# A two-stage FFT feeding a SoLU layer on one core: another order for the opening (x between the halves of w_in, Q in long rows, r by one-column products)

## The chip, the cores and the metric

The kernel runs on one core of one Trainium2 chip. The metric is the device time of one execution in microseconds (us), lower is better; the median of three runs is taken. One further execution was recorded by the profiler, and all views below come from it.

## What is computed

`x` is 8 x 3136 x 256 (float32). The first stage takes the real part of its two-dimensional FFT over the last two axes; the second treats the 25088 rows of the result as tokens of a SoLU layer:

```python
X = np.fft.fft(np.fft.fft(x, axis=1), axis=2).real      # 8 x 3136 x 256, then 25088 x 256
h = X @ w_in                                            # w_in 256 x 1024
e = np.exp(h - h.max(-1, keepdims=True))
solu = h * e / e.sum(-1, keepdims=True)
ln = (solu - mean(solu)) / sqrt(var(solu) + 1e-6) * g_ln
out = ln @ w_out                                        # w_out 1024 x 256
```

`w_in` and `w_out` arrive as float64. [...]each weight is loaded as two 32-bit words and put together on the core: the exponent is taken from the high word and clamped, the significand is formed from both words, and the two are multiplied into a float32.

## The kernel before, in words

**Tiling.** The sequence of 3136 = 49 x 64 is transformed in two steps. The batch of 8 is worked on as 4 pairs. For a pair, `load` (L108 on) brings in x in 8 chunks, c = 0 to 7: the rows `xa` by a direct load issued from SyncE (SP), L117, and the mirrored rows `xb` by an indirect load (gather) issued from GpSimd (POOL), L119. Each of the two is 98 partitions x 4 KB, 392 KB. VectorE (DVE) adds the mirror (`add_mirror`, L134 and L136) and folds the features (`fold`, L141, L142, L154) into `y`. TensorE (PE) multiplies `y` by the table `F` (`transform1`, L208), ScalarE (ACT) copies the result to `z` (L211), and SP stores it to a DRAM scratch `zd` (`keep`, L216), from where it is loaded again with the partitions in another order as `g` (`turn`, L224).

A **unit** is one of 100 sets of 128 or 256 tokens: one value of k1 (25 of them) in one of 4 pairs. For each unit `transform2` (L236) makes `q` (ACT copies it, L242), and `up` (L264) multiplies `q` by the combined weight `Wi` = Q w_in, where Q is the feature-FFT table. One feature column needs a rank-one term: `even` (L270) adds `w_mid` times a per-token scalar `r` to the product. `r` is one row of `q` laid over the 128 partitions; `spread` (L247) does that by a DMA that SP issues. Then follow, all on 128 x 1024 tiles: `join` (L278, DVE, twice: tokens k and mirrored k), `expo` (L286, ACT), `product` (L293, DVE), `square` (L300, ACT), a transposition, and the product with `w_out` (`down`, L468, or from unit 5 on a product of seven block products, L401).

**The weights.** Before the first unit can run, `w_in` must have been converted and multiplied by Q: `Wi` and `w_mid` come from `product_in(h)`, h = 0, 1, 2 (L601: four 128 x 512 matrix products each, two halves of the columns times two chunks of the depth). `w_in` is loaded and converted in four pieces of 128 x 512 (`piece_in` L504; `exponent_in` L507 and, on ACT, `confine` L529 to L531; `narrow_in` L507, L543, L546, L551). `w_out` is loaded in two halves (`load_out`, L613) and converted in four pieces (`exponent_out`, `narrow_out`, the same lines), with `g_ln` multiplied in at L551. `centre` (L631 to L633) then takes the mean out of `Wo`, and `weight_sums` (L377) makes the sums for the seven-product form.

**What sets the order.** The whole is in a manual schedule: each engine executes its instructions in the order in which the program text issues them. The opening is written out by hand (L672 to L758): idx and identity; piece 0 of w_in, then pieces and x chunks in turn, `F` after piece 1; Q and g_ln after x chunk 3 (g_ln as 128 x 8 single elements, Q as 2 x 257 elements for each partition); then for each chunk c the conversion of a piece (c = 0, 1, 2), the fold, the load of chunk c + 6, and the transform; `product_in(0)` after chunk 3; w_out, `load_table(0)` and `mid` in chunk 3's turn. Chunks 6 and 7 go to the two buffers that chunks 0 and 1 used, so their gathers wait for those folds. After the last chunk come the loads of `g`, the rest of the weights, units 0 to 3 (which use plain transposition on PE, `whole = 4`), and unit 4 as the first of the block-transposed form. From unit 6 on the loop repeats in a fixed pattern.

A compiled DMA signals its end on one of eight semaphores that SP uses in turn: in the compiled order of the SP queue each DMA waits for the one eight places before it.

Of the kernel before, what the change touches and what calls it, by code (L numbers as in the profile page):

```python
# [17 lines left out]
P = 128  # L18
# [10 lines left out]
KG = 5  # L29
# [6 lines left out]
def kernel(  # L36
# [139 lines left out]
    def transform1(pr, s):  # L176

        c, l = divmod(2 * s, CH)  # L180
        if s == 0:
            pr.zd = dram.tile([ZR, NH, D], FP32, tag="zd", name="zd")
        if l == 0:

            if pr.p or c < 2:
                pr.z = zpool.tile([ZR, CH, D], FP32, tag="z", name="z")
            elif c < 4:
                if c == 2:
                    pr.z_u = fpool.tile([P, 2, FF], FP32, tag="u", name="z_u", bufs=1)
                pr.z = pr.z_u[0:ZR, c - 2].rearrange("p (l d) -> p l d", l=CH)  # L190
            elif c < 6:
                pr.z = Ws.rearrange("p (h w) c k -> h p (w c k)", h=2)[c - 4, 0:ZR].rearrange("p (l d) -> p l d", l=CH)
            elif c == 6:
                pr.z = S_tiles[1][0:ZR, 0:2].rearrange("p a c k -> p (a c k)").rearrange("p (l d) -> p l d", l=CH)
            else:
                pr.z = gpool.tile([P, KG, D], FP32, tag="g", name="z_g")[0:ZR, 0:CH, :]
            pr.zs[c] = pr.z
        y = pr.y[c]
        ps = result(0 if pr.p else s).rearrange("p (l d) -> p l d", l=2)
        if s == NH // 2 - 1:  # L200
            parts = [(ps[0:ZR, 0], y[:, l], 0), (ps[0:ZR, 1], pr.y0[:, 0], 1), (ps[0:ZR, 1], y[:, l + 1], 2)]
        else:
            parts = [(ps[0:ZR], y[:, l : l + 2], 0)]
        pr.done.append(s)
        first = True
        for o, i, t in parts:
            for h, cs in enumerate((EVEN, ODD)):
                nc.tensor.matmul(o[..., cs], F[:, 2 * t + h, :], i[..., cs], start=first, stop=True,  # L208
                                 skip_group_check=True)
                first = False  # L210
        nc.scalar.copy(pr.z[:, l : l + 2, :], ps[0:ZR])  # L211
        if l == CH - 2:
            keep(pr, c, slice(0, ZR if pr.p else 4 * KG))
# [29 lines left out]

    def spread(t):

        t.r = small.tile([P, 1], FP32, tag="r", name="r")
        nc.sync.dma_start(out=t.r, in_=t.q[0:1, P : 2 * P])  # L247

    class Unit:


        def __init__(self, p, k1):
            self.p, self.k1 = p, k1
            self.signs = (0, 1) if k1 else (0,)
            self.h, self.u, self.ot = [None] * 2, [None] * 2, [None] * 2

    def up(t, c):
# [259 lines left out]
    def confine(unit, here=False):  # L519
# [11 lines left out]
        nc.scalar.activation(out=unit, in_=u, func=ACT.Identity, bias=limits[:, 2:3], scale=-(2.0 ** 23))  # L531

    def narrow(w, raw, outs, unit):

        if w.dtype == FP32:
            for o, scale in outs:
                nc.vector.tensor_scalar(out=o, in0=o, scalar1=scale, scalar2=2.0 ** 20, op0=ALU.mult, op1=ALU.mult)
            return
        lo, hi = raw[:, 0 : 2 * NW : 2], raw[:, 1 : 2 * NW : 2]

        bits(mantissa, hi, 0xFFFFF, ALU.bitwise_and, 0x100000, ALU.bitwise_or)
        m = lo.bitcast(FP32)
        nc.vector.scalar_tensor_tensor(out=m, in0=lo.bitcast(U32), scalar=2.0 ** -32, in1=mantissa, op0=ALU.mult,  # L543
                                       op1=ALU.add)

# [8 lines left out]
    class Weights:  # L554


        def load_in(self):
            raw = fpool.tile([P, 2, FF, 2], FP32, tag="v", name="raw_in", bufs=2)
            raw = raw.rearrange("p a f b -> p (a f b)").bitcast(I32)
            self.w_in = [fpool.tile([P, FF], FP32, tag="h", name="w_in", bufs=2) for _ in range(KD)]  # L560
            self.pieces, self.units = [], []
            for c in range(KD):
                for j in range(0, FF, NW):
                    i = 2 * (c * FF + j)
# [4 lines left out]

        def exponent_in(self, i):  # L570
            w, raw, o, c, j, n = self.pieces[i]
            self.units.append(exponent(w, raw))
            confine(self.units[-1])

# [4 lines left out]
        def load_tables(self):  # L579
            self.Q = fpool.tile([P, KD, D + 1], FP32, tag="ev", name="Q", bufs=1)  # L580
            nc.sync.dma_start(out=self.Q, in_=q_tab.rearrange("(c p) d -> p c d", p=P))
            nc.sync.dma_start(out=g_ln, in_=moe_g_ln.rearrange("(c p) -> p c", p=P))

# [5 lines left out]
        def mid(self):  # L589

            self.m = w_mid[:, 0 : KD * P].rearrange("p (c k) -> p c k", c=KD)
            for c in range(KD):
                nc.scalar.mul(out=self.m[:, c, :], in_=ones, mul=self.Q[:, c, D:])

        def product_in(self, h):
            ps = ps_h.tile([P, FF], FP32, tag=f"h{h % 2}", name="wps")
            for half in range(2):
                fs = slice(half * HW, (half + 1) * HW)
                for c in range(KD):
                    lhsT = self.m[:, c, :] if h == KD else self.Q[:, c, h * P : (h + 1) * P]  # L600
                    nc.tensor.matmul(ps[:, fs], lhsT, self.w_in[c][:, fs], start=(c == 0), stop=(c == KD - 1))  # L601
            nc.scalar.copy(w_mid if h == KD else Wi[:, h, :], ps)

# [12 lines left out]
        def scale_out(self):  # L616
            nc.scalar.mul(out=g_ln, in_=g_ln, mul=2.0 ** -20)

        def exponent_out(self, i):
            self.units.append(exponent(moe_w_out, self.raw[:, 2 * i * NW : 2 * (i + 1) * NW]))  # L620

        def narrow_out(self, i):
# [48 lines left out]
    with tc.manual_schedule():  # L671
# [6 lines left out]
        for c in range(2, 6, 2):  # L678
            room = fpool.tile([P, 2, KF, 4, 64], FP32, tag="uT", name="room", bufs=2)
            room = room[0:PR].rearrange("p w c i m -> p (w c i m)").rearrange("p (a n) -> p a n", a=4)  # L680
            rooms[c], rooms[c + 1] = [room[:, i] for i in (0, 1)], [room[:, i] for i in (2, 3)]
        weights.load_in()
        for c in range(4):
            weights.piece_in(c)
            if c:
                load(first, c - 1, rooms.get(c - 1))
            if c == 1:
                nc.sync.dma_start(out=F, in_=f_tab)
        load(first, 3, rooms[3])
        weights.load_tables()  # L690
        for c in range(4, 6):
            load(first, c, rooms[c])
        nc.vector.memset(ones, 1.0)
# [4 lines left out]
        for t in T:  # L698
            nc.vector.memset(t, 0.0)
        weights.exponent_in(0)  # L700
        weights.exponent_in(1)
        for c in range(NC):

            if c == 0:
                weights.narrow_in(0)
                weights.narrow_in(1)
            elif c < 3:
                weights.narrow_in(c + 1)
            if c < 2:
                weights.exponent_in(c + 2)  # L710
            add_mirror(first, c, nc.vector)
            fold(first, c)
            if c == NC - 1:
                for i in range(3):
                    weights.exponent_out(i)
            if c + 6 < NC:
                load(first, c + 6)
            if c == 3:
                weights.place_out()
                for i in range(2):  # L720
                    weights.load_out(i)
                weights.load_table(0)
                weights.mid()
                weights.scale_out()
            for s in range(CH // 2):
                transform1(first, c * CH // 2 + s)
            if c == 3:
                weights.product_in(0)

        turn(first, 0, nc.sync, 0, 2)  # L730
        turn(first, 0, nc.gpsimd, 2, KG)

        confine(weights.units[0], True)
        for i in range(1, 3):
            confine(weights.units[i])
        weights.product_in(1)
        weights.narrow_out(0)
        weights.exponent_out(3)
        weights.product_in(2)
        for i in range(1, 3):  # L740
            weights.narrow_out(i)

        units = [Unit(p, k1) for p in range(NP) for k1 in range(NK)]
        for t in units[:2]:
            take2(t, transform2(pairs[0], t.k1))
            spread(t)
        confine(weights.units[-1])
        for c in (2, 3, 0, 1, 4, 5, 6, 7):
            keep(first, c, slice(4 * KG, ZR))
        weights.load_table(1)  # L750
        lag = 5
        whole = 4

        def second_transform(i):
            if i < len(units):
                t = units[i]
                take2(t, transform2(pairs[t.p], t.k1))
                spread(t)  # L758

# [6 lines left out]
        def begin(i):  # L766

            cur = units[i]
            enter(i)
            even(cur, up(cur, 0))  # L770
            cur.odd = up(cur, 1)
# [7 lines left out]
        batches = []  # L779
        begin(0)  # L780
        for i in range(whole + 1):
# [14 lines left out]
            if i == 0:  # L796

                weights.narrow_out(3)
            for s in cur.signs:
# [112 lines left out]
def _tables(B, S, D):  # L912
# [13 lines left out]
    for t, (u, v) in enumerate(tabs):  # L926
# [18 lines left out]
    rows = np.arange(B)[:, None, None] * S + (N1 - np.arange(1, NK)) + N1 * np.arange(N2)[::-1, None]  # L945
    mirror[:, B // 2 * NC :] = rows.reshape(B // 2, P, NK - 1).transpose(1, 0, 2).reshape(P, -1)
    return {
        "f_tab": f.reshape(PR, 6, ZR).astype(np.float32),
# [37 lines left out]
```

## Time and profile before

| what | us |
|---|---|
| median of three runs (lowest, highest) | 1158.69 (1158.67, 1158.85) |
| profiled execution: own time | 1157.6 |
| profiled execution: span of the core | 1155.8 |
| outside the span in that execution | 1.8 |
| PE busy in the span | 1109.1 (96%) |
| DVE busy | 1013.8 (88%) |
| POOL busy | 848.0 (73%) |
| ACT busy | 758.3 (66%) |
| x of the first pair folded (start of L507 behind the last L154) | 46.68 |
| first `even` (L270), of unit 0 | 59.62 |
| `even` of unit 2 | 77.95 |
| first of the PE instructions that then follow each other to the end | 113.84 |

How to read it: busy times are sums over the whole span, so they say little of the first 114 us, where this change lies. Times of single events are counted from the start of the span. "Chain of work that ended last" is a path that the profile follows back from the last instruction, at each step to what released it. A DMA queue named q1 is the one that SP issues to, q0 the one that POOL issues to; both run on the same 16 DMA engines.

### The profile page before, as it was taken

How to read it: one execution, taken by the hardware profiler on the slowest of the kernel's cores; microseconds unless marked ns; L12 is line 12 of the kernel's file. 1: busy time of each engine (PE TensorE's matmuls, PEld its weight loads, DVE VectorE, ACT ScalarE, POOL GpSimd, SP SyncE). 2: the span in 40 equal slices, each digit the busy share in tenths (PEclk: the TensorE clock that was granted, in tenths of full speed). 3: DMA queues.
4: the chain of work that ended last, by engine and by line, in shares of the span. 5: the costliest groups of instructions: out<-in, count | busy, mean ns of one | idle time of the engine just before them, and what ended most of it. 6: DMA issues, size and time to landing. Idle time of an engine off the chain costs nothing.

```text
span 1155.8 us, 21664 instructions
## 1 busy us (share of the span) xinstructions
PE 1109.1 (96%) x7026; PEld 888.2 (77%) x7026; DVE 1013.8 (88%) x1440; ACT 758.3 (66%) x1725; POOL 848.0 (73%) x742
## 2 busy tenths in 40 slices
PE   2888999999999999999999999999999999999998
PEld 1555787888887778878887778878778788888887
DVE  7879988888999998888899998888898999898883
ACT  4567667666665766666666766666666676676661
POOL 3035888865898988866689888877499596777764
PEclk9999999999999999999999999999999999999999
DMA  9771798766998779866969697876697675865664
GB/s 238 204 192 39 168 191 195 184 145 145 160 187 160 180 177 184 198 138 143 164 139 204 150 189 171 203 175 141 149 159 146 137 163 122 150 144 111 139 135 111
DMA packets 458479, 185.75 MB, mean 161 GB/s; under 512 B 425750, under 2 KB 440350, under 8 KB 458368
## 3 DMA queue, kind: packets, MB, share of 16 engines
q1 hardware_dynamic: 444608, 146.22, 61.2%
q0 software_dynamic: 13760, 38.16, 12.4%
q8 instruction: 57, 0.93, 0.3%
q14 instruction: 54, 0.44, 0.1%
HBM read 44.78 MB, written 38.80 MB: 72 GB/s over the span
## 4 chain that ended last, share of the span: by engine, by line
PE 81%; DMA 5%; SPq 4%; DVE 4%; issue 2%; POOL 2%; ACT 1%; POOLq 0%; DVEq 0%; ACTq 0%
PE ps_m L401 48%; PE ps_h L264 25%; PE ps_m L208 4%; PE ps_m L236 3%; SPq L365 3%; DMA room<-in_x_dram 2%; DMA uT<-v 1%; DVE h L278 1%; POOL S L394 1%; DMA r<-q 1%; DVE u L293 1%; DMA F<-in_f_tab_dram 1%; SPq L216 1%; PE ps_m L468 1%; PE wps L601 1%
## 5 line engine op out<-in xcount | busy, mean ns | idle before, releaser
L264 PE MATMUL ps_h<-Wi,q 128*128 128x512 f32 x800 | 362.0, 594 | 7.9 <-DVE nmax L278 4.8
L394 POOL TENSOR_TENSOR S<-uT 128x512 f32<-128x512 f32 x186 | 251.1, 1350 | 104.6 <-DMA out_dram<-ot 40.9
L300 ACT ACTIVATE h<-u,usum 128x1024 f32<-128x1024 f32 x196 | 225.2, 1149 | 139.9 <-DVE u L293 139.9
L401 PE MATMUL ps_m<-Ws,S 128*128 128x128 f32 x2304 | 298.7, 276 | 4.3 <-issue 3.0
L401 PEld LDWEIGHTS ps_m<-Ws,S 128*128 128x128 f32 x2304 | 280.8, 192 | 8.8 <-issue 3.3
L264 PEld LDWEIGHTS ps_h<-Wi,q 128*128 128x128 f32 x800 | 144.0, 190 | 155.3 <-issue 139.9
L293 DVE SCALAR_TENSOR_TENSOR u<-h,u 128x1024 f32<-128x1024 f32 x196 | 259.4, 1359 | 0.8 <-ACT u L286 0.7
L286 ACT ACTIVATE u<-h,nmax 128x1024 f32<-128x1024 f32 x196 | 223.6, 1143 | 15.8 <-DVE nmax L278 11.8
L336 DVE STREAM_TRANSPOSE v<-u 128x2048 f32<-128x2048 f32 x93 | 215.5, 2317 | 3.2
L401 PE MATMUL ps_m<-Wo,uT 128*128 128x128 f32 x1536 | 213.1, 282 | 0.0
L401 PEld LDWEIGHTS ps_m<-Wo,uT 128*128 128x128 f32 x1536 | 197.3, 197 | 0.9 <-issue 0.9
L394 POOL TENSOR_TENSOR S<-uT,S 128x512 f32<-128x512 f32 x93 | 133.1, 1431 | 7.3
L278 DVE CUSTOM_DVE_ANT_0 h<-ev,ps_h 128x1024 f32<-128x1024 f32 x100 | 122.1, 1221 | 17.3 <-DVE ev L270 7.9
L479 POOL DMA_INDIRECT out_dram<-ot,idx x96 | 111.2, 1158 | 33.5 <-issue 16.6
L394 POOL TENSOR_TENSOR S<-S,uT 128x512 f32<-128x512 f32 x93 | 126.6, 1362 | 7.3
L278 DVE CUSTOM_DVE_ANT_0 h<-h,ps_h 128x1024 f32<-128x1024 f32 x96 | 117.3, 1221 | 14.2 <-ACT ot L444 0.5
L270 DVE SCALAR_TENSOR_TENSOR ev<-w_mid,r,ps_h 128x1024 f32<-128x1024 f32 x100 | 124.0, 1240 | 4.2 <-DMA r<-q 2.3
L401 PE MATMUL ps_m<-Ws,uT 128*128 128x128 f32 x768 | 106.2, 281 | 0.0
L401 PE MATMUL ps_m<-Wo,S 128*128 128x128 f32 x768 | 102.0, 276 | 0.7 <-ACT ot L435 0.7
L316 POOL TENSOR_TENSOR rs<-v,neg_half 128x2 f32<-128x2 f32 (+1 forms) x100 | 78.2, 782 | 28.4 <-ACT v L309 27.0
L236 PEld LDWEIGHTS ps_m<-T,g 128*128 128x128 f32 x400 | 60.1, 191 | 49.4 <-issue 45.8
L401 PEld LDWEIGHTS ps_m<-Ws,uT 128*128 128x128 f32 x768 | 98.0, 196 | 0.0
(96 smaller groups left out, 1135.5 us busy)
## 6 DMA issues: line engine op xcount, KB each, us to landing
uT<-v SPq DMA_DIRECT2D x752, 128.0 KB
out_dram<-ot SPq DMA_DIRECT2D x100, 128.0 KB
g<-zd POOLq DMA_DIRECT2D x72, 160.0 KB, 5.2
xa<-in_x_dram SPq DMA_DIRECT2D x28, 392.0 KB
zd<-z SPq DMA_DIRECT2D x24, 400.0 KB
raw_in<-in_moe_w_in_dram SPq DMA_DIRECT2D x4, 512.0 KB
raw_out<-in_moe_w_out_dram SPq DMA_DIRECT2D x2, 1024.0 KB
r<-q SPq DMA_DIRECT2D x100, 0.5 KB
```

The source lines that it names most:

```text
L236: nc.tensor.matmul(o, g[:, k, h * P : (h + 1) * P], table, start=(h == 0), stop=True, skip_group_check=True)
L264: nc.tensor.matmul(ps[:, fs], t.q[:, c * P : (c + 1) * P], Wi[:, c, fs], start=True, stop=True)
L270: nc.vector.scalar_tensor_tensor(out=t.ev, in0=w_mid, scalar=t.r, in1=ps, op0=ALU.mult, op1=ALU.add)
L278: nc.vector.tensor_tensor_reduce(out=t.h[s], in0=t.h[0] if s else t.ev, in1=t.odd, scale=1.0 if s else -0.5, scalar=3.0e38, op0=ALU.add, o ...
L286: nc.scalar.activation(out=t.u[s], in_=t.h[s], func=ACT.Exp, bias=t.nmax[:, s : s + 1], scale=-1.0, accum_out=t.esum[:, s : s + 1])
L293: t.last = nc.vector.scalar_tensor_tensor(out=t.u[s], in0=t.h[s], scalar=-1.0, in1=t.u[s], op0=ALU.mult, op1=ALU.mult, accum_out=t.usum[:, ...
L300: nc.scalar.activation(out=t.h[s], in_=t.u[s], func=ACT.Square, bias=t.usum[:, s : s + 1], scale=-float(FF), accum_out=t.ssq[:, s : s + 1])
L316: nc.gpsimd.tensor_tensor(out=t.rs[:, n], in0=t.v[:, n], in1=neg_half[:, n], op=ALU.pow)
L336: nc.vector.transpose(out=t.batch.v[:, t.w].rearrange("p f o -> p o f"), in_=t.both)
L394: i = engine.tensor_tensor(out=S[j], in0=a, in1=b, op=op)
L401: nc.tensor.matmul(o, a[:, c], b[:, c], start=start and c == 0, stop=c == n - 1, skip_group_check=True)
L479: dma = nc.gpsimd.indirect_dma_start(out=out, out_offset=bass.IndirectOffsetOnAxis(ap=idx[:, i : i + 1], axis=0), in_=t.ot[s], in_offset=None)
```

## The change

Only the opening is changed, up to unit 4; the loop from unit 5 on is the same text.

1. **Order of the loads.** The pieces of w_in are numbered by halves of the columns (first both depth chunks of columns 0 to 511, then of 512 to 1023). Pieces 0 and 1 are loaded first, then all of x, with F, Q and g_ln after chunk 0. Chunks 6 and 7 get a buffer of their own (`room_v`), so their gathers wait for nothing. Pieces 2 and 3 are issued after the stores of chunks 2 and 3, and w_out after the last chunk, its first half ahead of the loads of `g` on SP and its second half behind them.
2. **Q and g_ln.** The table Q is stored so that a partition is one row of 514 elements. g_ln is loaded as 8 rows of 128 elements and turned by a product with the identity on PE (L637 of the new text).
3. **Conversion.** `narrow` is split: the significand (the mask and the L546 of the new text) becomes `significand`, called ahead of it. Pieces 2 and 3 of w_in are converted after the last fold, their exponents clamped by DVE in place of ACT. Of w_out, piece 0 is converted before unit 0, piece 1 inside unit 0, pieces 2 and 3 inside unit 1 (before: pieces 0 to 2 ahead of unit 0 and piece 3 inside it).
4. **product_in** works on one half of the columns: the first halves of the three products lie behind chunks 0, 1 and 2, the second halves behind the last chunk, cut again by depth: three products of depth 0, the second transform of unit 0, three products of depth 1. `m`, the mean vector's operand, gets its own tile.
5. **r.** For units 0 to 3 `spread` is replaced by `column`: a product of the row of `q` with a single 1 gives a 128 x 1 column in PSUM, which DVE copies to `r`. Units 4 and later keep the DMA.

```diff
+    def column(t):
+        ps = result(2)[:, 0:1]
+        nc.tensor.matmul(ps, t.q[0:1, P : 2 * P], ones[0:1, 0:1], start=True, stop=True)
+        t.r = small.tile([P, 1], FP32, tag="r", name="r")
+        nc.vector.tensor_copy(out=t.r, in_=ps)
...
+    def significand(w, raw):
+        lo, hi = raw[:, 0 : 2 * NW : 2], raw[:, 1 : 2 * NW : 2]
+        bits(mantissa, hi, 0xFFFFF, ALU.bitwise_and, 0x100000, ALU.bitwise_or)
+        nc.vector.scalar_tensor_tensor(out=lo.bitcast(FP32), in0=lo.bitcast(U32), scalar=2.0 ** -32, in1=mantissa,
+                                       op0=ALU.mult, op1=ALU.add)
...
-            nc.sync.dma_start(out=self.Q, in_=q_tab.rearrange("(c p) d -> p c d", p=P))
-            nc.sync.dma_start(out=g_ln, in_=moe_g_ln.rearrange("(c p) -> p c", p=P))
+            nc.sync.dma_start(out=self.Q, in_=q_tab.rearrange("p (c d) -> p c d", c=KD))
+            self.g8 = fpool.tile([P, D], FP32, tag="ot", name="g8", bufs=6)[0:KF, 0:P]
+            nc.sync.dma_start(out=self.g8, in_=moe_g_ln.rearrange("(c p) -> c p", p=P))
...
+        def product_in(self, h, half, depth=range(KD)):
+            fs = slice(half * HW, (half + 1) * HW)
+            if depth[0] == 0:
+                if half and h == KD:
+                    self.sums[h] = result(3)[:, 0:HW]
+                else:
+                    self.sums[h] = ps_h.tile([P, FF], FP32, tag=f"h{h % 2}", name="wps")[:, fs]
+            for c in depth:
+                lhsT = self.m[:, c, :] if h == KD else self.Q[:, c, h * P : (h + 1) * P]
+                nc.tensor.matmul(self.sums[h], lhsT, self.w_in[c][:, fs], start=(c == 0), stop=(c == KD - 1))
+            if depth[-1] == KD - 1:
+                nc.scalar.copy(w_mid[:, fs] if h == KD else Wi[:, h, fs], self.sums[h])
...
+        for i in range(2):
+            weights.piece_in(i)
+        for c in range(6):
+            load(first, c, rooms.get(c))
+            if c == 0:
                 nc.sync.dma_start(out=F, in_=f_tab)
+                weights.load_tables()
...
+        for i in range(2):
+            weights.exponent_in(i)
+        for i in range(2):
+            weights.significand_in(i)
+            weights.narrow_in(i)
         for c in range(NC):
             add_mirror(first, c, nc.vector)
             fold(first, c)
             for s in range(CH // 2):
                 transform1(first, c * CH // 2 + s)
+            if c == 0:
+                weights.mid()
+            if c < 2:
+                load(first, c + 6, rooms[c + 6])
+            elif c < 4:
+                weights.piece_in(c)
+            elif c == 4:
+                weights.load_table(0)
+            if c < 1 + KD:
+                weights.product_in(c, 0)
+        weights.place_out()
+        weights.load_out(0)
         turn(first, 0, nc.sync, 0, 2)
         turn(first, 0, nc.gpsimd, 2, KG)
+        weights.load_out(1)
+        weights.scale_out()
+        for i in (2, 3):
+            weights.exponent_in(i, True)
+            weights.significand_in(i)
+            weights.narrow_in(i)
+        for i in range(2):
+            weights.exponent_out(i)
         confine(weights.units[0], True)
+        weights.significand_out(0)
         weights.narrow_out(0)
...
+        for h in (0, KD, 1):
+            weights.product_in(h, 1, range(1))
+        second_transform(0)
+        for h in (0, KD, 1):
+            weights.product_in(h, 1, range(1, KD))
+        confine(weights.units[0])
...
+        enter(0)
+        ps = up(units[0], 0)
+        column(units[0])
+        even(units[0], ps)
+        weights.significand_out(1)
+        units[0].odd = up(units[0], 1)
+        second_transform(1)
+        second_transform(2)
+        for c in (2, 3, 0, 1, 4, 5, 6, 7):
+            keep(first, c, slice(4 * KG, ZR))
+        weights.load_table(1)
...
             if i == 0:
-                weights.narrow_out(3)
+                weights.narrow_out(1)
+                for j in (2, 3):
+                    weights.exponent_out(j)
+                    confine(weights.units[-1])
+            if i == 1:
+                for j in (2, 3):
+                    weights.significand_out(j)
+                    weights.narrow_out(j)
```

## The prediction

> **What bounds the kernel now.** I read the chain of work that ended last, in order of time, first:
>
> ```profile
> 2.63 8.52 DMA F<-in_f_tab_dram
> 11.15 0.02 issue
> 11.17 24.83 DMA room<-in_x_dram
> ...
> 69.61 8.23 DMA r<-q
> ...
> 113.84 1.11 PE ps_m L208 x4
> 114.95 3.62 PE ps_m L401 x32
> ```
>
> Up to 36 us the chain is loads, then mostly VectorE (DVE) work, and from 113.84 on PE instruction after PE instruction. The table by stage, cut at the last fold (46.8), at the `even` of unit 2 (77.95) and at 113.84, agrees:
>
> ```profile
> 0.00:46.80 46.80, 22.52 (x66) 13.72 (x67) 35.66 (x73) 19.51 (x31) 9.04 (x14) 1.00 0.94 251
> 46.80:77.95 31.15, 28.24 (x116) 17.28 (x114) 24.54 (x42) 20.71 (x39) 8.24 (x9) 1.00 0.68 174
> 77.95:113.84 35.89, 28.35 (x122) 17.16 (x123) 34.15 (x48) 26.45 (x57) 18.27 (x20) 1.00 0.21 51
> 113.84:1155.80 1041.96, 1029.97 (x6724) 840.02 (x6724) 919.49 (x1280) 691.60 (x1600) 812.42 (x701) 1.00 0.75 160
> ```
>
> The columns are the stage, its length, busy time of PE, PE weight load, DVE, ACT, POOL, then clock, DMA share and GB/s. Stage one is full on the DMA side (0.94), stage three on DVE (34.15 of 35.89), stage four on PE (1029.97 of 1041.96). The change ends before stage four, so what it moves is the start of that stage, one for one, if stage three, whose DVE order is nearly the same, is passed on unchanged. So I ask when `even` of unit 2 starts (77.95 now). What DVE waits for up to 113.84:
>
> ```profile
> DVE S L507 <- DMA raw_in<-in_moe_w_in_dram: 6.2, 4, 2.3
> DVE room L134 <- DMA room<-in_x_dram: 3.1, 1, 3.1
> DVE ev L270 <- DMA r<-q: 2.3, 1, 2.3
> DVE ev L270 <- ACT S L530: 1.9, 1, 1.9
> ```
>
> The third line is the prize of part 5: 2.3 us, once. The second is x chunk 4, late. SP's timeline says why:
>
> ```profile
> 9.06 0.39 SPq L582 DMA_DIRECT2D g_ln<-in_moe_g_ln_dram  x1
> 11.17 17.04 SPq L117 DMA_DIRECT2D room<-in_x_dram  x2
> 28.33 0.33 SPq L117 DMA_DIRECT2D xa<-in_x_dram  x1
> ```
>
> Behind the g_ln load the issue of two x loads takes 17 us (one of them 15.995); xa of chunks 6 and 7 goes out only at 28.3 and 29.2. The DMA engines are nevertheless at work all that time. From 28 to 32 us:
>
> ```profile
> DMA packets 950, 0.72 MB, mean 181 GB/s; under 512 B 667, under 2 KB 810, under 8 KB 950
> ...
> q0 software_dynamic: 182, 0.56, 65.9%
> q1 hardware_dynamic: 768, 0.16, 30.7%
> ```
>
> So 181 GB/s where 11.5 to 16 us has 257: small packets on q1, and q0 (the gathers) ahead.
>
> **What the Trainium skill says.** "DMA: Bandwidth & Descriptors", Rules for kernel authors: a last dimension that isn't contiguous becomes one descriptor per element; g_ln is 1024 such, and the 667 packets under 512 B agree. The same page, Queues, rings and completion order: each DMA engine takes turns between the queues that have work. The trace agrees: from 11.5 to 16 us q0 has 51.7% and q1 50.6%. The same page, Why a DMA increments its semaphore by 16 and not by 1: a DMA runs on the largest number of engines up to 16 that divides its outer size, so 98 partitions use 14. No view shows engines singly; w_out's 388 GB/s (40 to 44 us) against 292 for x alone (36 to 40) points that way. "TensorE: Matmul & The Clock Gate", Part 1: after idling PE runs at half clock for some 3.4 us; the first transforms here take 3.73 us for 8 products, later 1.94.
>
> **The change part by part.** Let E be the end of the last fold (now 46.68).
>
> *x earlier.* Until F lands (11.15) the new order moves the same as now. After that q0 has the rest of eight gathers: the first lands at 14.0 (issue 3.01, 11.0 to landing), the next at 17.5 and 21.0, so 3.5 us each while q1 is busy, and 2.85 of 3.5 us of the first are left: 7.8 gathers. q1 has seven xa, Q and two small stores. A gather with an xa beside it is 2 x 0.40 MB in 3.5 us, 229 GB/s. At that rate 7.8 x 0.40 + 7 x 0.40 + 0.26 + 0.16 = 6.35 MB takes 27.7 us: 38.9. At the 257 GB/s measured with w_in pieces in the mix it would be 24.7: 35.9. The two-sided bound is 35.9 to 38.9; I take 38.0, since the last xa runs without a partner (1.6 us each, from chunks 4 to 6 now). The cost of Q's short rows and g_ln's single elements is in this difference. DVE follows: 2.6 us a fold against 3.5 us between chunks. The last fold costs 43.88 to 46.68 = 2.8, so E = 40.8, 5.9 us earlier.
>
> *What is late next.* Pieces 2 and 3 of w_in are now behind E. Rows of the DVE timeline, start to start: exponent 0.40, two clamps 0.80, mask 0.45, L543 0.61, L546 0.78, last product 0.69: 3.73 each, done at E+3.75 and E+7.45 (their loads follow x by about 3.5 us at w_out's rate, in time). Then two exponents 0.80, two clamps 0.80, piece 0 of w_out 2.65: E+11.8 with the `r` copy; its load, issued at E+3.1 and 2.7 us long at 388 GB/s, lands at about E+7.9, so E+12.2.
>
> PE is later still. Three products of depth 0 (0.86 each: 3.44 us for 4) end at E+6.4. `transform2` of unit 0 waits for `g`: the last store is at E+2.8 (49.49 now), the SP loads of `g` start 1.94 later, and w_out's 1 MB stands ahead of them on q1 until about E+7.4. Now `g` is there by E+8.9 at the latest (PE reads it at 55.55), so E+8.1 to E+9.3, I take E+8.8. Behind that wait stand 0.4 for the transform, three depth-1 products 2.6, `up` 1.7, `column` and its DVE copy 0.4: `even` of unit 0 at E+13.9 = 54.7 (59.62 now, E+12.9). `column` is in no trace; it has one column where the 128 x 128 form takes 0.27 us, and a DVE read of 128 x 1 is 0.08, so 0 to 0.4; I take 0.4 on PE's path here, 0.12 on DVE later.
>
> *Units 0 and 1.* Now 77.95 - 59.62 = 18.33 from `even` 0 to `even` 2. Off: the r wait 2.31, two short waits 0.38 and 0.30. On: two exponents 0.80 and two whole pieces of w_out (2 x 2.65; piece 1 takes the place of piece 3), two copies 0.24. Sum 21.7. The ACT clamps inside lie beside DVE. `centre` still waits for the last piece, as now.
>
> So `even` of unit 2 starts at 40.8 + 13.9 + 21.7 = 76.4, 1.5 us earlier; unit 3's copy takes 0.1 back. Forecast: 1.4 us off. The span becomes 1154.4, the profiled execution's own time 1156.2, and 1158.69 - 1.4 = 1157.3 for the median, as the profiled execution lies 1.1 us below it. The DMA of `r` for four units leaves SP: 0.5 us of issue each, hidden now except for the one wait. The zd stores and the second table are issued earlier on SP, with nothing waiting.
>
> **Rivals.** About 0.2% (2.3 us) is what a measurement of this kernel can tell from no change.
>
> *A, clearly faster.* x lands at 35.9 and `g` isn't delayed by w_out, so that DVE alone sets unit 0: E = 38.7, `even` 0 at E+12.2, `even` 2 at 72.6: 5.3 off, 1153.4. For it: 257 GB/s was sustained from 9 to 20 us. Against it: only w_in's pieces load all engines.
>
> *B, slower.* x isn't earlier by enough to pay for the work put behind it. The mechanism is the mix of two x streams on 14 engines, the place is chunks 3 to 7 between 20 us and E. The price: pieces 2 and 3 (7.5 us) and w_out's pieces (6.1) were in DVE's idle time before, 5.3 us of it between 46.68 and 77.95, and now follow E on the path. With E + 35.6 + 0.1 for 77.95, it decides from E = 42.25; over 0.2% needs E above 44.55, chunk 7 landing after 41.7. For it: a gather and a chunk of xa at times took 3.5 us together with engine shares already over 100%, and slow engines may lag. Typical time: E = 45.2, 1161.6.
>
> *C, the r wait doesn't go.* `column` shares a PSUM bank with the transposed tiles that ACT copies out, and PE and then DVE would wait for those in place of the DMA: 2.3 back, so 1158.69 - 1.4 + 2.3 = 1159.6. Against it: the copies of unit 1 (L356, 87.6 to 88.7) end before unit 3's second `up` starts (89.58).
>
> **How the numbers follow.** Forecast 0.52, A 0.26, B 0.17, C 0.05. Forecast and C are within 0.2%, but the forecast's upper end crosses the bound with 0.04. So faster 0.30, same 0.52, slower 0.18. The forecast's own range, from E of 39.0 to 42.3 and 1 us on `g`, is 1155.0 to 1159.5. The range for 8 in 10 reaches half way into A and to the foot of B: 1154.2 to 1160.8.
>
> **What would show it.** SP has no long issue between 11 and 28 us; chunk 7's fold starts at 38 to 39 and ends at E = 40.8; PE waits for `g` after the depth-0 products; `even` 0 at E+13.9, `even` 2 at 76.4, with no wait on `r`; the PE sequence starts at 112.4. It is wrong if E is above 42.3, if DVE waits for w_in's second half, or if stage three gets longer.

## The result, and the profile after

The changed kernel takes 1164.12 us (median of 14 runs, 1159.2 to 1170.23); the kernel before, run beside it, 1158.6 us (14 runs, 1153.88 to 1160.41). The medians are 5.5 us apart. The ratio goes by the means (1164.02 and 1157.58 us): 1.0056, 95% interval 1.0038 to 1.0073, so 6.4 us slower. The forecast was 1157.3 us, with a range up to 1160.8. The profiled execution of after has an own time of 1161.38 us and a span of 1159.6, so it shows 3.8 of the 6.4 us.

The table by stage of after, cut at the same events as before's (the columns as there):

```profile
0.00:40.30 40.30, 20.75 (x69) 12.83 (x70) 29.95 (x62) 16.16 (x26) 9.14 (x14) 1.00 0.92 243
40.30:58.22 17.92, 14.14 (x40) 6.92 (x39) 11.49 (x27) 5.03 (x11) 2.33 (x4) 0.81 0.83 265
58.22:80.80 22.58, 16.60 (x58) 9.63 (x57) 20.42 (x34) 13.21 (x25) 3.56 (x4) 0.92 0.61 169
80.80:117.91 37.11, 31.61 (x148) 19.93 (x146) 34.37 (x49) 28.67 (x63) 20.44 (x21) 1.00 0.08 17
117.91:1159.60 1041.69, 1029.85 (x6724) 840.00 (x6724) 920.47 (x1280) 691.81 (x1600) 814.95 (x701) 1.00 0.75 160
```

E, the end of the last fold, is at 40.30: 6.4 us earlier, as wanted. It is lost again in the next two stages and more: from E to the first `even` DVE is busy for 11.49 of 17.92 us, and PE's clock (third number from the end) is 0.81 and then 0.92, where every stage of before had 1.00. (The record of the granted clock begins at 20.8 us in after and at 34.5 in before; the table counts what lies ahead of that as full clock, though the first transforms of before took 3.73 us for 8 products there, later ones 1.94.) The last stage is unchanged (1041.69 against 1041.96). Side by side:

| | before | after | difference | forecast difference |
|---|---|---|---|---|
| E | 46.68 | 40.30 | -6.4 | -5.9 |
| E to `even` of unit 0 | 12.9 | 17.9 | +5.0 | +1.0 |
| to `even` of unit 2 | 18.3 | 22.6 | +4.3 | +3.4 |
| to the PE sequence | 35.9 | 37.1 | +1.2 | +0.1 |
| start of the PE sequence | 113.84 | 117.91 | +4.1 | -1.4 |

What DVE waits for up to that start:

```profile
DVE r L264 <- PE ps_m L262: 4.2, 1, 4.2
DVE room L134 <- DMA room<-in_x_dram: 4.1, 4, 1.3
...
DVE h L285 <- ACT h L307: 2.2, 3, 1.3
DVE S L514 <- DMA raw_out<-in_moe_w_out_dram: 1.6, 1, 1.6
```

The 2.3 us for `r` by DMA are gone. In their place stand 4.2 us for `r` by PE, once, ahead of unit 0. The column itself takes 0.38 us on PE; the rest of the wait is everything that is late on PE before it. PE's timeline behind the last fold (start, length, what; in brackets the idle time before it):

```profile
44.15 1.54 PE L619 MATMUL wps<-w_in,Q 128*128 128x512 f32 x2 [1.53 <-DVE w_in L562]
45.49 1.91 PE L619 MATMUL ps_m<-w_in,m 128*128 128x512 f32 x2
47.20 1.50 PE L619 MATMUL wps<-w_in,Q 128*128 128x512 f32 x2
50.93 0.68 PE L236 MATMUL ps_m<-T,g 128*128 128x128 f32 x4 [2.24 <-DMA g<-zd]
51.45 1.80 PE L619 MATMUL wps<-w_in,Q 128*128 128x512 f32 x2
53.05 1.92 PE L619 MATMUL ps_m<-w_in,m 128*128 128x512 f32 x2
54.76 1.13 PE L619 MATMUL wps<-w_in,Q 128*128 128x512 f32 x2
55.73 1.88 PE L271 MATMUL ps_h<-Wi,q 128*128 128x512 f32 x4
57.54 0.38 PE L262 MATMUL ps_m<-ones,q 1*128 1x1 f32 x2
```

`g` is there at E+10.6 (forecast E+8.8), and the three depth-1 products take 4.3 us from start to start instead of 2.6: rows of 1.9 are products at half clock, rows of 1.0 at full, and the trace records half clock from 44.7 to 48.1 us and from 51.6 to 55.0. Why `g` is late stands in SP's timeline:

```profile
43.11 0.27 SPq L216 DMA_DIRECT2D zd<-z_g  x1
43.56 0.40 SPq L632 DMA_DIRECT2D raw_out<-in_moe_w_out_dram  x1
45.03 1.74 SPq L224 DMA_DIRECT2D g<-zd  x4
```

1 MB of w_out is issued between the last store and the loads of `g`. From that store's issue to the transform are 7.8 us. Before has no such load there, and 6.1 us (its transform starts at 55.55):

```profile
49.49 0.27 SPq L216 DMA_DIRECT2D zd<-z_g  x1
51.43 1.73 SPq L224 DMA_DIRECT2D g<-zd  x4
```

### The profile page after: what moved, and what is told of

Same layout as the page of the kernel before. It is cut to its first block, busy times and chain, and to the rows that moved or that the text cites. A ratio compares the mean times of both kernels' runs of the same rounds, so it can differ in the third digit from the quotient of the medians.

```text
span 1159.6 us, 21674 instructions
## 1 busy us (share of the span) xinstructions
PE 1113.0 (96%) x7035; PEld 889.3 (77%) x7035; DVE 1016.7 (88%) x1448; ACT 754.9 (65%) x1722; POOL 850.4 (73%) x742
## 3 DMA queue, kind: packets, MB, share of 16 engines
q0 software_dynamic: 13760, 38.16, 12.2%
## 4 chain that ended last, share of the span: by engine, by line
PE 84%; DVE 4%; DMA 4%; ACT 2%; issue 2%; SPq 2%; POOL 1%; POOLq 0%; DVEq 0%; ACTq 0%
PE ps_m L408 49%; PE ps_h L271 26%; PE ps_m L208 4%; PE ps_m L236 3%; DMA room<-in_x_dram 2%; SPq L372 1%; DVE h L285 1%; DVE u L300 1%; ACT h L307 1%; POOL S L401 1%; DMA xa<-in_x_dram 1%; PE ps_m L475 1%; DMA uT<-v 1%; DVE ev L277 0%; DMA g<-zd 0%
## 5 line engine op out<-in xcount | busy, mean ns | idle before, releaser
L486 POOL DMA_INDIRECT out_dram<-ot,idx x96 | 112.1, 1168 | 33.9 <-issue 17.1
L285 DVE CUSTOM_DVE_ANT_0 h<-h,ps_h 128x1024 f32<-128x1024 f32 x96 | 117.2, 1221 | 15.5 <-ACT h L307 2.0
```

What stands on the lines that cost most here:

```text
L285: nc.vector.tensor_tensor_reduce(out=t.h[s], in0=t.h[0] if s else t.ev, in1=t.odd, scale=1.0 if s else -0.5, scalar=3.0e38, op0=ALU.add, o ...
L486: dma = nc.gpsimd.indirect_dma_start(out=out, out_offset=bass.IndirectOffsetOnAxis(ap=idx[:, i : i + 1], axis=0), in_=t.ot[s], in_offset=None)
```

## The experiments

All ratios are to the kernel before, run beside each kernel. "After" stands at 1.0056 and was not run again beside the experiments, so a gain over it is the difference of two ratios. By the widths of the intervals such a difference is known to about 2.4 us (an estimate): a gain of 3.3 us is clear of that, one of 2.5 or 2.8 barely, one of 1.7 not. e5, e6 and e8 have 5, 6 and 4 runs, the others 13 to 22. In the profiled executions (us; the last columns are the three stretches of the table above):

| kernel | ratio, 95% interval | E | to even 0 | to even 2 | to PE sequence |
|---|---|---|---|---|---|
| before | 1 | 46.7 | 12.9 | 18.3 | 35.9 |
| after | 1.0056 [1.0038, 1.0073] | 40.3 | 17.9 | 22.6 | 37.1 |
| e1 w_out earlier | 1.0027 [1.0016, 1.0039] | 41.9 | 16.0 | 22.6 | 36.1 |
| e2 PE kept busy | 1.0032 [1.0020, 1.0043] | 42.5 | 17.4 | 22.6 | 36.1 |
| e5 clamps later | 1.0041 [1.0028, 1.0054] | 40.3 | 18.1 | 21.8 | 36.9 |
| e6 piece 1 first | 1.0034 [1.0022, 1.0046] | 40.3 | 17.9 | 21.8 | 36.1 |
| e7 all four | 1.0002 [0.9993, 1.0012] | 40.6 | 15.6 | 20.6 | 36.5 |
| e9 the order alone | 1.0003 [0.9991, 1.0016] | 40.1 | 16.1 | 20.6 | 36.1 |
| e10 e9, PE busy behind folds | 1.0006 [0.9996, 1.0017] | 42.4 | 15.7 | 20.6 | 36.1 |
| e11 ACT clamps, piece 2 first | 1.0002 [0.9991, 1.0013] | 40.5 | 19.3 | 17.2 | 36.9 |
| e12 ACT clamps | 0.9991 [0.9980, 1.0003] | 40.8 | 13.8 | 21.1 | 36.4 |
| e3 before + column | 1.0002 [0.9988, 1.0016] | 47.1 | 13.4 | 16.1 | 36.1 |
| e4 before + long rows | 1.0009 [0.9995, 1.0023] | 49.1 | 12.9 | 16.0 | 35.9 |
| e8 w_in inside the folds | 1.0111 [1.0096, 1.0126] | 50.3 | 18.1 | 20.7 | 36.5 |

The theory after the result: three small orders behind E cost the time (w_out ahead of `g`, a piece of w_out inside unit 0, ACT's clamps in front of a square), and half-clock windows of PE add to it. The rivals: one part, the column or the long rows, is slow by itself; or the whole idea (x ahead of the second half of w_in) is wrong.

**e1: w_out's first half issued in chunk 5's turn,** ahead of the last chunks' stores, so that nothing stands between them and `g`.

```diff
+            elif c == 5:
+                weights.place_out()
+                weights.load_out(0)
...
-        weights.place_out()
-        weights.load_out(0)
         turn(first, 0, nc.sync, 0, 2)
```

> The changed kernel with the first half of w_out issued on SP in chunk 5's turn, so that it no longer stands ahead of the loads of g. Theory (the end of the opening is set by PE: g late behind w_out, then half-clock windows after idling): g lands 2 to 3 us sooner after the last store (6 us in place of 7.7), even of unit 0 starts 2 to 4 us sooner than E+17.9, and the time falls to about 1161.5. Rival (the work put behind the last fold on DVE is the whole cost): PE's wait for g has no effect, time stays at about 1164.

1.0027: 2.9 thousandths, 3.3 us, less than after. SP's rows of this kernel, then one of PE's:

```profile
44.72 0.28 SPq L216 DMA_DIRECT2D zd<-z_g  x1
47.14 1.73 SPq L224 DMA_DIRECT2D g<-zd  x4
```

```profile
50.65 0.68 PE L236 MATMUL ps_m<-T,g 128*128 128x128 f32 x4 [2.05 <-DMA g<-zd]
```

From the last store to the transform are 5.9 us now (after: 7.8), and DVE's wait for `raw_out` is gone. In the profile E is 1.6 later, so `even` 0 comes only 0.3 earlier, and the depth-1 products still take 4.3, in a half-clock window from 51.6 to 55.0. w_out in front of `g` is a cause; of the three it has the largest gain, but the intervals don't tell the three apart.

**e2: PE kept busy,** by eleven more 128 x 512 products that nothing uses (`busy(n, ...)` issues n of them): six around the depth-0 products, five in the centring.

```diff
+        busy(2, 1, weights.w_in[0][:, 0:HW])
         for h in (0, KD, 1):
             weights.product_in(h, 1, range(1))
+        busy(4, 1, weights.w_in[0][:, 0:HW])
         second_transform(0)
...
+            busy(3, 3, Wi[:, 0, 0:HW])
             for c in range(KF):
-                nc.tensor.matmul(cs, ones, Wo[:, c, :], start=(c == 0), stop=(c == KF - 1))
+                nc.tensor.matmul(cs, ones, Wo[:, c, :], start=(c == 0), stop=(c == KF - 1), skip_group_check=True)
+                if c in (3, 5):
+                    busy(1, 3, Wi[:, 0, 0:HW])
```

> The changed kernel with eleven products of 128x512 added whose results nobody reads: two ahead of the depth-0 products, four ahead of the second transform of unit 0, five around the sum over w_out (centre). They add 9.5 us of PE work, most of it where PE waits. Theory (half-clock windows follow idle windows of PE): no half-clock record between 40 and 80 us, the depth-1 products take 2.6 in place of 4.3 us, and the time falls by 2 to 3 us, to about 1161.5, with less spread. Rival (DVE work alone): as the changed kernel, 1164, or a little above it.

1.0032. The depth-1 products run at full clock, 1.02 each:

```profile
50.52 3.60 PE L262 MATMUL ps_m<-w_in,ones 128*128 128x512 f32 x8
54.38 0.68 PE L236 MATMUL ps_m<-T,g 128*128 128x128 f32 x4 [0.27 <-DMA g<-zd]
54.90 1.02 PE L624 MATMUL wps<-w_in,Q 128*128 128x512 f32 x2
55.76 1.02 PE L624 MATMUL ps_m<-w_in,m 128*128 128x512 f32 x2
56.62 1.02 PE L624 MATMUL wps<-w_in,Q 128*128 128x512 f32 x2
```

The mean clock of its runs is 0.9975, of after's 0.9923. In the profiled execution the gain doesn't show (its half-clock windows fell into the folds, E 42.5, and `g` came at E+11.8), so the 2.8 us rest on the ratio.

**e5: the six ACT clamps of w_out's pieces 2 and 3 behind the square of unit 0** instead of in front of it.

```diff
-                    confine(weights.units[-1])
...
+            if i == 0:
+                for unit in weights.units:
+                    confine(unit)
```

> The changed kernel with ACT's six clamps for w_out pieces 2 and 3 issued behind the square of unit 0 in place of ahead of it. Theory (they hold up the square, and with it the second join of unit 1, by 1.3 us): that wait of L285 on ACT goes, even of unit 2 starts 1.3 us sooner after even of unit 0 (21.3 in place of 22.6), 1162.5 against 1164 where the kernel before has 1157.5. Rival (unit 1 is held by PE's sum over w_out, which the same clamps no longer delay in the same way): no change.

1.0041: 1.5 thousandths, 1.7 us, less than after, which by itself is not clear of noise. The rows of ACT and DVE in after that led to it:

```profile
63.65 0.72 ACT L536 ACTIVATE S<-S,limits 128x512 f32<-128x512 int32 x1 [0.66 <-DVE S L514]
...
67.91 1.13 ACT L307 ACTIVATE h<-u,usum 128x1024 f32<-128x1024 f32 x1
```

```profile
69.17 1.22 DVE L285 CUSTOM_DVE_ANT_0 h<-h,ps_h 128x1024 f32<-128x1024 f32 x1 [1.31 <-ACT h L307]
```

ACT clamps for 4.3 us, then squares, and DVE's next join waits 1.31 for that. With the edit this wait is at most 0.5, and `even` 0 to `even` 2 falls from 22.6 to 21.8.

**e6: piece 1 of w_out converted ahead of unit 0,** clamped by DVE, not inside unit 0.

```diff
-        confine(weights.units[0], True)
-        weights.significand_out(0)
-        weights.narrow_out(0)
+        for unit in weights.units:
+            confine(unit, True)
+        for i in range(2):
+            weights.significand_out(i)
+            weights.narrow_out(i)
...
-        confine(weights.units[0])
...
-        weights.significand_out(1)
...
-                weights.narrow_out(1)
```

> The changed kernel with piece 1 of w_out converted ahead of unit 0, where DVE waits 4.2 us for the column of r, in place of inside unit 0. Theory (DVE idles there because PE is late, so work there is free, and inside the units it is on the path): even of unit 0 starts at the same distance from the last fold, unit 0 is 2.6 us shorter, the time falls by about 2.6 us (0.22%). Rival (the cost is DVE's work as such, wherever it stands between the last fold and unit 2): no change.

1.0034: 2.2 thousandths, 2.5 us, less than after. DVE's waits in this kernel:

```profile
DVE S L514 <- DMA raw_out<-in_moe_w_out_dram: 1.5, 1, 1.5
...
DVE r L264 <- PE ps_m L262: 0.8, 1, 0.8
```

The piece falls into the wait for the column, 4.2 in after and 0.8 now; `even` 0 is not later (58.16 against 58.22). But unit 0 does not become 2.6 shorter: the stretch to `even` 2 falls by 0.8 only, because without the piece DVE waits there for ACT's exponential, which it did not in after:

```profile
DVE u L300 <- ACT u L293: 1.3, 1, 1.3
```

Another 1.0 is gained behind `even` 2, so the profile shows 1.8 in all (start of the PE sequence 116.10 against 117.91).

**e3 and e4: one part alone on the kernel before.** e3 takes part 5 (`column` in place of `spread` for units 0 to 3), e4 part 2 (Q and g_ln in long rows).

```diff
...
     take2(t, transform2(pairs[t.p], t.k1))
-    spread(t)
+    if i >= whole:
+        spread(t)
...
     ps = up(cur, 0)
+    if i < whole:
+        column(cur)
```

> The kernel before with part 5 alone, r of units 0 to 3 by a one-column product. Theory: the 2.3 us wait of even of unit 2 on r goes and nothing takes its place but a 0.16 us copy for each unit; 1156.5. Rival (PE waits for the copies out of the shared PSUM bank, or unit 2 is then held by PE): 1158.6.

> The kernel before with part 2 alone, Q and g_ln in long rows. Theory: no 16 us issue on SP, DVE's 3.05 us wait for chunk 4 shrinks, the last fold ends 2 to 3 us sooner than 46.68 and the start of the PE sequence follows: 1156. Rival (the 16 DMA engines are full anyway, so x comes no sooner): 1158.6.

Both level with before: 1.0002 and 1.0009. So neither is the slow part, but neither earns anything by itself either. In e3 the wait for r by DMA is gone and `even` 0 to `even` 2 is 2.2 shorter, yet the mean span of its 14 runs is that of the kernel before (1154.73 both), and its interval ends at 0.9988, where 2.3 us off every run would be 0.9980. In e4, which keeps the DMA, that stretch is 16.0 too, with no wait for r. So the 2.3 us of before's profile are not a price that every run pays. In e4 two x loads are issued in 4.4 us instead of 17, and E is still later than in before (49.1). DVE's waits in e4:

```profile
DVE S L507 <- DMA raw_in<-in_moe_w_in_dram: 6.8, 4, 2.7
DVE room L134 <- DMA room<-in_x_dram: 2.8, 2, 2.5
DVE y L141 <- PE ps_m L208: 2.3, 1, 2.3
```

The first two add up to what before has (6.2 and 3.1). The third is new, and is about the 2.4 us by which E is later: PE is at half clock up to 41.1 us in this execution (before: 34.5), and the fold waits until it has read `y`. So this profile does not tell how early x could have been folded; that the long rows alone gain nothing rests on the ratio.

**e7: e1, e2, e5 and e6 together, and e8: as e7, but w_in's second half loaded behind chunks 1 and 2** and converted and multiplied between the folds, so that nothing of it is left behind E.

```diff
             load(first, c, rooms.get(c))
+            if c in (1, 2):
+                weights.piece_in(c + 1)
...
             fold(first, c)
+            if c in (2, 3):
+                weights.exponent_in(c)
+                weights.significand_in(c)
+            if c in (3, 4):
+                weights.narrow_in(c - 1)
...
-            elif c < 4:
-                weights.piece_in(c)
...
+            elif c > 4:
+                weights.product_in((0, KD, 1)[c - 5], 1)
```

> The changed kernel with four of its parts mended together: first half of w_out issued in chunk 5's turn, PE kept busy by eleven unused products, the six clamps behind the square, piece 1 of w_out ahead of unit 0. Theory: the gains add up to 3 + 2 + 1.3 + 2.6, less where they overlap: 7 us below the changed kernel, that is level with the kernel before or 0.1% under it. Rival (one bound behind all): no more than the best single one, 3 us.

> As the four mended together, and the second half of w_in loaded behind chunks 1 and 2 of x, converted behind the folds of chunks 2 to 4 and multiplied behind chunks 5 to 7, so that nothing of w_in is left behind the last fold. Theory (what stands behind the last fold is the cost): the last fold ends 2 to 3.5 us later than in the changed kernel, even of unit 0 follows it by 11.5 to 12.5 in place of 17.9 us, and the time is 3 to 5 us below the kernel before. Rival (x first is what gains): slower than the four mended alone by the 3 us that x comes later.

e7 is level with before, 1.0002, as expected. e8 is 1.1% slower, where a gain was expected. Its waits and some of its PE rows:

```profile
DVE room L134 <- DMA room<-in_x_dram: 8.8, 2, 5.2
DVE r L269 <- PE ps_m L267: 4.8, 1, 4.8
DVE S L519 <- DMA raw_out<-in_moe_w_out_dram: 4.3, 1, 4.3
```

```profile
35.39 3.70 PE L208 MATMUL ps_m<-y,F 98*100 98x258 f32 x8 [4.06 <-DVE y L154]
40.77 3.70 PE L208 MATMUL ps_m<-y,F 98*100 98x258 f32 x8 [1.68 <-DVE y L154]
```

x is late (waits of 5.2 and 3.6), the conversions stand between the folds, PE goes to half clock (3.70 for 8 products of the transform that take 1.89 at full clock; half clock is recorded from 33.5 to 50.6) and E is 50.3, 10 us later than in after, where 2 to 3.5 had been expected. Nor does the stretch behind E become shorter, 18.1 where about 12 had been expected: DVE waits 4.3 for w_out and 4.8 for the column. So with w_in's second half ahead of E nothing is gained in this form, and the rival that the idea of part 1 is wrong finds no support. How much of the 10 us is due to the loads, to the conversions and to the clock was not separated.

**e9 and e10: which of the four mendings count.** e9 is e7 without the unused products; e10 has only the six behind the folds.

> The version with all four mendings, but without its 11 unused products: only the three changes of order (w_out's first half issued earlier, six ACT clamps behind the square of unit 0, piece 1 of w_out converted ahead of unit 0). Theory (half-clock windows are a cost of their own, set by PE's idle time behind the last fold and in the centring): 2 to 3 us above the version with the products, a ratio to before of 1.0015 to 1.0030, with half-clock windows between 45 and 80 us in the profile. Rival (the order alone fills the idle time, and the unused products only take PE time): level with before within 0.1%, no such window or one at most.

> The three changes of order and only the six unused products around the depth-0 products of w_in's second half; the five in the centring of w_out are left out. If the windows behind the folds are what costs: level with before, as with all eleven (ratio 0.9995 to 1.0010). If the one in the centring (about 75 us) costs as much: 1.0010 to 1.0020, with one half-clock window between 68 and 80 us.

1.0003 and 1.0006: the rival of e9's expectation holds. With the order mended, the unused products bring nothing, though the mean clock of e9's runs is only 0.9943 (e7's 0.9970; before's, run beside e9, 0.9978). A half-clock window is in e9's profile too (49.3 to 52.7), and two depth-1 products take 1.92 and 1.79; but DVE now has work at that time:

```profile
DVE r L264 <- PE ps_m L262: 0.6, 1, 0.6
```

So in this profile the window costs at most those 0.6 us on the way to `even` 0, because DVE's path is nearly the last. That windows cost nothing in e9 at all is not shown: over its 14 runs a lower clock still goes with a longer span (correlation -0.77, about 0.8 us for each 0.001 of the clock). Why its mean is nevertheless that of e7, with more clock, stays open.

**e11 and e12: a try at beating both.** To e9 is added that ACT, idle from 42.9 to 49.7 in e9, clamps w_in's piece 3 and w_out's pieces 0 and 1 in place of DVE; e11 also moves piece 2 of w_out ahead of unit 0.

```diff
-        for i in (2, 3):
-            weights.exponent_in(i, True)
-            weights.significand_in(i)
-            weights.narrow_in(i)
-        for i in range(2):
-            weights.exponent_out(i)
-        for unit in weights.units:
-            confine(unit, True)
-        for i in range(2):
-            weights.significand_out(i)
-            weights.narrow_out(i)
+        weights.exponent_in(2, True)
+        weights.exponent_in(3)
+        weights.significand_in(2)
+        weights.narrow_in(2)
+        weights.significand_in(3)
+        for i in range(2):
+            weights.exponent_out(i)
+            confine(weights.units[-1])
+        weights.narrow_in(3)
+        for i in range(2):
+            weights.significand_out(i)
+        for i in range(2):
+            weights.narrow_out(i)
...
```

> The three changes of order, and ACT's idle time behind the last fold used: it clamps the exponents of w_in's piece 3 and of w_out's pieces 0 and 1 (nine instructions of 0.73 us, in a stage in which ACT is busy for 3.4 of 15.8 us), in place of DVE (3 x 0.89 = 2.7 us less). The time that DVE gains takes piece 2 of w_out (0.42 + 0.89 + 0.42 + 0.69 + 0.75 + 0.88 = 4.0), which leaves unit 1. Theory (from the last fold on DVE's busy time plus its idle time is the time; PE's path to the first even, 16 us, is fixed): the first even 0 to 1.5 us later, even of unit 2 2 to 3 us earlier, 1.5 to 3 us below the version with the order alone, ratio to before 0.9975 to 0.9990. Rival (ACT's clamps stand ahead of the copy of q and PE's path gets longer): 1.0000 to 1.0015.

> The same, but piece 2 stays inside unit 1: DVE only has 2.7 us less to do ahead of the first even, and waits that much longer for the column. Theory: level with the version of the order alone and with before, 0.9995 to 1.0010, and DVE's wait for the column 3 us in the profile where it was 0.65. If DVE's work ahead of unit 0 is what sets the first even, 0.9980 to 0.9990.

e11 is level with before, 1.0002, and misses what was expected: `even` 0 is 3.2 later behind E than in e9, which takes back the 3.4 that the next stretch gains. DVE now waits for w_out's second half, issued behind `g`.

```profile
55.63 0.43 DVE L514 TENSOR_SCALAR S<-raw_out 128x512 int32<-128x512 int32 x1 [2.39 <-DMA raw_out<-in_moe_w_out_dram]
```

e12 is the best of all, 1156.14 us and 0.9991, but its interval reaches 1.0003: perhaps a tenth of a per cent, not settled, and between the two outcomes that its expectation names. Its PE rows are those that the forecast had assumed for after:

```profile
49.01 0.68 PE L236 MATMUL ps_m<-T,g 128*128 128x128 f32 x4 [1.21 <-DMA g<-zd]
49.53 1.02 PE L619 MATMUL wps<-w_in,Q 128*128 128x512 f32 x2
50.39 1.02 PE L619 MATMUL ps_m<-w_in,m 128*128 128x512 f32 x2
51.24 1.02 PE L619 MATMUL wps<-w_in,Q 128*128 128x512 f32 x2
```

`g` at E+8.2, products at full clock, `even` 0 at E+13.8 (forecast for after: E+13.9). DVE waits 0.9 for the column, not 3: the expectation had left PE's path at e9's length.

## Why the prediction was wrong

**Right: x earlier.** E was forecast at 40.8 and is 40.30, with 243 GB/s in that stage, inside the assumed 229 to 257. The mechanism held; that the number came within half a microsecond is partly luck, since E lies between 40.1 and 42.5 in the profiles of the experiments that keep this order (e1 to e12 without e3, e4 and e8). The conversion of w_in's second half behind it ends at 47.8, E+7.5 as forecast. The column is 0.38 us on PE (bound 0.4) and 0.16 on DVE (forecast 0.12), and rival C (its bank) shows nowhere. The wait for `r` by DMA is gone.

**The step that failed: `even` of unit 0 at E+13.9.** It came at E+17.9. The sum was that of PE's path, and two of its terms were too small:

- `g` at E+8.8, measured E+10.6: 1.8 us. The prediction saw w_out's 1 MB ahead of `g` and still put `g` where the kernel before has it without that load in front (E+8.9). w_out itself is in use only at E+9.1 (forecast E+7.9). e1, which takes that 1 MB away, shortens store to transform by 1.9 and the time by 3.3.
- Depth-1 products 2.6, measured 4.3: 1.7 us, and another 0.4 on what follows. The prediction named the Trainium skill's "TensorE: Matmul & The Clock Gate", Part 1, and then priced every product at full clock. In before, 7 us of products lay between the transforms of x and `g` without a gap (first rows below). After has only three products there, and gaps of 1.5 and 2.2 us. The page's closing section, Why this matters for your kernels, allows gaps up to about 3 us; here the measurement decides: half-clock windows followed the shorter ones too, the 1.5 not in every kernel (last section).

```profile
48.68 3.60 PE L601 MATMUL wps<-w_in,Q 128*128 128x512 f32 x8
52.12 3.60 PE L601 MATMUL wps<-w_in,w_mid 128*128 128x512 f32 x8
55.55 0.61 PE L236 MATMUL ps_m<-T,g 128*128 128x128 f32 x4
```

That DVE's 1.6 us for `raw_out` came in addition cost nothing, since DVE then still waited 4.2 for PE. The deeper fault is that DVE's path (forecast E+12.2, measured 53.7 = E+13.4) and PE's were compared, and 1.7 us of idle DVE were accepted while a whole piece of w_out (2.65 us) was left inside unit 0. e6 fills that gap: 2.5 us by the ratios, 1.8 in the profile.

**Units 0 and 1: 21.7 forecast, 22.6 measured.** "The ACT clamps inside lie beside DVE" is the term that failed: they stand in front of a square for which the next join waits, 1.31. e5 takes 0.8 off this stretch.

**Stage three: +0.1 forecast, +1.2 measured.** From `even` of unit 2 to that of unit 3 are 8.67 us in after and 7.62 in e1, e2, e6 and e9 (before: 7.43). Here the prediction's own sign of being wrong came true: stage three got longer. In after DVE waits there 0.68 us for a square of ACT and 0.42 for an exponential, in e9 for neither. In after a half-clock window lies from 75.5 to 78.9, over the end of the centring and `up` of unit 2; in e5 two from 69.4 to 76.2, with 8.45 us. But e7 takes 8.04 with no window at all, and e1 7.62 with one at 68.7. The clock may be part of what makes ACT late; the cause stays open.

**Rival B had the sign, not the mechanism.** It decided from E = 42.25, by x being late; E was 40.3. But its price, the conversions that now follow E, is what a ledger of DVE's busy and idle time shows. Up to E, DVE is busy for 35.66 us in before and for 29.95 in after: of the 6.4 us by which E is earlier, 5.7 are work that was moved behind it, and DVE's idle time ahead of E is nearly the same (11.1 and 10.4). Up to the PE sequence DVE is busy 94.35 us and idle 19.5 in before, busy 96.23 and idle 21.7 in after: 1.9 more work (two pairs of clamps moved from ACT to DVE, 0.89 each) and 2.2 more idle, 4.1 together. e9 has 97.28 and 15.5, e12 94.94 and 17.2. An early E alone could gain 0.7 us; the rest would have had to come from less idle time behind it, and there was more.

**How it adds up.** e1, e6 and e5 take 3.3, 2.5 and 1.7 us off after, 7.5 as a sum of the single ones and 6.1 together (e9). Together the three orders account for all of the loss within the intervals; the share of each is known only roughly. On the mean the clock is no fourth part beside them: e2 takes 2.8 us off after, but once the orders are mended the same products bring nothing (e7 against e9). What stays open is how the 3.8 us of after's profiled execution and the 6.4 of its mean divide among the windows: the other runs have no trace. Their granted clocks (0.988 to 0.997) and spans run together, correlation -0.8, about 1 us for each 0.001. That would fit half-clock windows on PE's path: by an estimate one window of 3.41 us lowers the mean clock of such a span by 0.0015 and delays PE by up to 1.7 us.

## What to carry to other kernels

An event that comes earlier because work was moved behind it is no gain: keep a ledger of busy and idle time of the bounding engine up to the point that counts, and ask of every idle stretch that is left what could be put into it. When work is taken away in front of a DMA wait, PE can lose both its cover and its clock; price the products behind the wait at half speed (1.9 us in place of 1.0 each here), and keep a large load out of the queue in front of the small one that the path waits for.

## What had not been expected of the hardware

As the traces record the granted clock, half-clock windows last 3.413 us each (the one at the program's end apart), and their starts lie multiples of that apart. Cutting PE's rows of all the traces at these times, up to 115 us, shows after which windows half clock followed. Where PE, at full clock, was busy for less than 1.4 us of a window, it followed each time (twelve windows, two of them in after, with 1.2 us each). Where PE was busy for 1.9 us or more, it never did. In between it did both: half clock followed 1.88 us in after and in e6 and 1.55 in e11, but not 1.88 in e5, 1.75 in e9 and 1.49 in after. So there is no sharp limit in these figures; e12, with 2.0 us of work where after had 1.9, was past it. That the spread of one program, 1159.2 to 1170.2 us in after, comes from where the windows fall fits the clocks of its runs, but is not shown.

The early stage, where DMA is 0.92 busy, is not free of PE's clock either: in e4 DVE's fold waited 2.3 us for PE at half clock. In e2 and e10 half-clock windows fell into the folds too (33.2 to 43.4 and 33.9 to 40.7), and E was at 42.5 and 42.4 us. But there DVE waited only 0.4 us for PE, and more than 2 us longer than in after for x; e1 had E at 41.9 with no such window.
